# Moving the SiLU-derivative passes of a backward kernel, and weaving one weight-gradient block into the transform

## The chip, the core and the metric

The kernel runs on one core of a Trainium2 chip. The metric is device time in microseconds (us) of one execution; lower is better. The engines named below are TensorE (PE, matmuls), its weight loads (PEld), VectorE (DVE), ScalarE (ACT), GpSimd (POOL) and SyncE (SP), which here only issues DMA transfers. Each engine takes its own list of instructions in order. A tile framework builds these lists ahead of time from the program's dependencies, its priorities and explicit `issue_after` edges, so the order of the source is not always the order on an engine.

## What is computed

The program is the forward and backward pass of four residual blocks: two long-convolution blocks (done by FFT) and two dense blocks with SiLU, in turn.

```python
def _B_ref(x, w1, w2):
    h = jnp.einsum("bsd,df->bsf", x, w1)      # S=2048, D=448, F=1792
    h = _silu(h)
    return jnp.einsum("bsf,fd->bsd", h, w2)

x = A_q
x = x + _A_ref(_layernorm(x), A_k, A_v, A_shift_k, A_ssm_k, A_ssm_D)   # long convolution
x = x + _B_ref(_layernorm(x), B_w1, B_w2)                              # dense, "layer 1"
x = x + _A_ref(_layernorm(x), A_k, A_v, A_shift_k, A_ssm_k, A_ssm_D)
x = x + _B_ref(_layernorm(x), B_w1, B_w2)                              # dense, "layer 2"

_out, _vjp = jax.vjp(_f, A_q, A_k, A_v, A_shift_k, A_ssm_k, A_ssm_D, B_w1, B_w2)
return (_out, *_vjp(grad_out))
```

In the backward pass of a dense block, the gradient at the hidden layer is `(g @ w2.T) * silu'(h)`. The kernel keeps the pre-activation `h` (tiles `dT`; for layer 1 stored to memory as `DT_d` and loaded back as `dTl`) and turns it into `silu'(h)` in place with an ACT pass, the "derivative pass".

## The kernel before

The sequence is cut into four chunks of 512 rows. `L == 1` is layer 2, `L == 0` is layer 1. For each chunk of the backward pass, `ga` forms `g @ w2.T` (matmuls into `ps_g`, an ACT copy to `ghp`, a DVE multiply with the derivative into `ghT`), and `gn` multiplies by `w1.T` (matmuls into `ps_n`, evacuated by ACT into `lb_u0`) and runs the layer-norm gradient on DVE, for four row tiles `tl`. `g_pre` transposes the incoming gradient on PE (`ps_t`) and copies it out (`gT`).

```python
    def slope(self, d):                       # derivative passes over one half chunk
        for o in range(0, 7, 2):
            n = min(2, 7 - o)
            self.nc.scalar.activation(d[:, o:o + n, :], d[:, o:o + n, :], ACT.Derivative_silu)
        self.k.bal.add("act", 3.4)

    def h(self, c, L, nT, half, hold, pre=None):
        ...                                   # pre-activations in ps_h; ACT: Silu into aT; DVE: copy into dT
            last = nc.scalar.activation(a, ps[:, 0:n, :], ACT.Silu)
        ...
        if L == 1:
            if half == 1:
                with self.tc.issue_after(last.ins):
                    for _, d in hold:
                        self.slope(d)

    def ga(self, c, L, gT, dT, mid=None, loads=(None, None)):
        ...
        for fp in range(NF // 2):             # 7 pairs of hidden blocks
            ps = k.psum.tile([P, 2, 512], FP32, name="ps_g", tag="mm", bufs=2)
            self.contract(ps, self.w2T, gT, 2 * fp, 2, ...)
            gh = self.ch.tile([P, 2, 512], BF16, name="ghp", tag="ghp", bufs=2)
            k.last_gh = nc.scalar.copy(gh[:], ps[:])
            if fp == 2 and mid:
                with self.tc.issue_after(k.last_gh.ins):
                    mid()
            ...                               # DVE: ghT = dT * gh
            if fp in (3, 6):
                hh = (fp - 3) // 3
                if loads[hh]:
                    ld.append(self.load_d(*loads[hh]))      # dTl <- DT_d, three buffers "D"
                self.store_turned(k.GH_d[L], ghT[hh], c, hh)  # DMA transposes on SP's queue

    def gn(self, c, L, ghT, nb, gres, na):
        for tl in range(4):
            pn = k.psum.tile([P, 512], FP32, name="ps_n", ...)
            for ft in range(NF):
                nc.tensor.matmul(pn[:, :D], lhsT=ghT[ft // 7][...], rhs=self.w1T[:, ft, :], ...)
            u0 = self.ch.tile([P, D], FP32, name="lb_u0", tag="lb_u0", bufs=2)
            last_u = nc.scalar.activation(u0[:], pn[:, :D], ACT.Identity, scale=..., accum_out=...)
            if tl == 1:
                k.mid_u = last_u
            ...                               # DVE: layer-norm gradients (ln_bwd twice), gYb

    def run(self):
        ...
        for c in range(4):                    # layer 2, forward end and backward
            gb, gT = self.g_pre(c, 1, gb_next if c else self.g_load(0))
            d0 = self.h(c, 1, nT, 1, cur, (lambda: self.load_d(0, 0)) if c == 3 else None)
            ...
            self.out(c, cur, True)
            ...
            if c == 3:
                self.slope(d0)
            ...                               # ga(c, 1, ...)
            if c == 3:
                ...
                nl = self.load_n(0)
                gn = self.g_pre(0, 0)
            self.gn(c, 1, ghT, nb, lambda tl: gb[:, tl, :], na)
        for c in range(4):                    # layer 1, backward
            with self.tc.issue_after(k.mid_u.ins):
                self.slope(d1)
            ...
            ghT = self.ga(c, 0, gT, dT, (lambda: self.slope(e0)) if c < 3 else None, ...)
            if c < 3:
                ...
                gn = self.g_pre(c + 1, 0)
            self.gn(c, 0, ghT, nb, lambda tl: self.X[:, 4 * c + tl, :], na)
```

After that comes the suffix: the FFT of the gradient `gYb` and the weight gradients. `_gw2` is a generator of matmuls (`ps_d`), 32 for each of 14 blocks of the gradient of `w2`; `_gw1` does the same for `w1`. `weave(n)` places `n` of these matmuls on PE between pieces of the transform, and the rest is drained near the end.

```python
        for _ in _gw2(k, k.dp, range(1), [(k.dp, "dstat", 3)], first=k.go_jobs.ins):
            pass                              # the first block, in one piece

        def jobs():
            yield from _gw2(k, k.dp, range(1, NF), both)
            yield from _gw1(k, dp2, both)
        ...
        for n2 in range(16):                  # first stage of the transform: 2 matmuls, 1 copy each
            with _in_turn(k):
                _fft_stage1(k, n2, k.gYb[:, n2, :], A1, psum, nc.scalar if n2 < 12 else None)
            weave(2 if n2 < 8 else 8 if n2 < 12 else 12)
```

Of the kernel before, what the change touches and what calls it, by code (L numbers as in the profile page):

```python
# [12 lines left out]
ACT = mybir.ActivationFunctionType  # L13
# [451 lines left out]
class Main:  # L465
# [91 lines left out]

    def slope(self, d):
        for o in range(0, 7, 2):
            n = min(2, 7 - o)  # L560
            self.nc.scalar.activation(d[:, o:o + n, :], d[:, o:o + n, :], ACT.Derivative_silu)  # L561
        self.k.bal.add("act", 3.4)

# [99 lines left out]

    def gn(self, c, L, ghT, nb, gres, na):
        nc, k = self.nc, self.k
# [4 lines left out]
        for tl in range(4):  # L670
            t = 4 * c + tl
            pn = k.psum.tile([P, 512], FP32, name="ps_n", tag="tr" if L == 1 and tl % 2 else "po", bufs=2)
            for ft in range(NF):
                nc.tensor.matmul(pn[:, :D], lhsT=ghT[ft // 7][:, ft % 7, tl * P:(tl + 1) * P], rhs=self.w1T[:, ft, :], start=(ft == 0), stop=(ft == NF - 1))  # L674
            u0 = self.ch.tile([P, D], FP32, name="lb_u0", tag="lb_u0", bufs=2)
            last_u = nc.scalar.activation(u0[:], pn[:, :D], ACT.Identity, scale=k.rstd[2 * L + 1][:, t:t + 1], accum_out=cp[:, tl, 0:1])  # L676
# [38 lines left out]
    def run(self):  # L715
        k, nc = self.k, self.nc
        pairs = ((0, 2), (2, 4))
        with self.tc.high_priority():
            self.a_fwd(0, 0, k.x0c0, k.na0, pairs)
            nT = self.b_tr(self.b_pre(0, 1, pairs, nc.vector))  # L720
        cur = []
        self.h(0, 0, nT, 0, cur)
        for c in range(4):
# [13 lines left out]
        for c in range(4):  # L737
# [10 lines left out]
            if c == 3:  # L748
                self.slope(d0)
            box = []  # L750
            if c < 3:
                ghT = self.ga(c, 1, gT, cur, lambda: box.append(self.b_pre(c + 1, 3)))
            else:
                ghT, d1, e0 = self.ga(c, 1, gT, cur, None, ((0, 1), (1, 0)))
# [5 lines left out]
            else:  # L760
                k.GO = k.wk.tile([P, NT, D], BF16, name="GO", tag="WA")
                k.go_jobs = k.d_load
                nl = self.load_n(0)
                gn = self.g_pre(0, 0)
            self.gn(c, 1, ghT, nb, lambda tl: gb[:, tl, :], na)
            na, nb = na1, nb1
        for c in range(4):
            with self.tc.issue_after(k.mid_u.ins):
                self.slope(d1)
            dT, (nb, na), (gb, gT) = ((None, d0), (None, d1)), nl, gn  # L770
            ghT = self.ga(c, 0, gT, dT, (lambda: self.slope(e0)) if c < 3 else None, ((c + 1, 1) if c < 3 else None, (c + 2, 0) if c < 2 else None))
# [32 lines left out]
def _job(k, ps, src, ft, mov, slot, start, stop, first=None):  # L804
# [6 lines left out]
    for t in range(NT):  # L811
        i = k.nc.tensor.matmul(ps[:, :D], lhsT=st[:, t, :], rhs=mov[:, t, :], start=start and t == 0, stop=stop and t == NT - 1)  # L812
        k.pe_engine = i.ins.engine
        yield i
# [46 lines left out]
def _ssm_suffix(k):  # L861
# [7 lines left out]
    with ExitStack() as es:  # L869
# [229 lines left out]
```

## Time and profile before

| what | value |
|---|---|
| device time, median of 3 runs | 764.16 us (762.78 to 764.94) |
| span of the profiled execution | 764.7 us |
| PE busy | 714.1 us (93%) |
| DVE busy | 510.2 us (67%) |
| ACT busy | 459.6 us (60%) |
| mean granted TensorE clock | 0.984 of full speed |

A busy share is an average over stages; what a stage is limited by is read from that stage's own time line. In such a line stand the start in us from the start of the span, the length in us, the engine, the source line and operation, the tile written and the tile read, how many instructions were merged, and in square brackets the idle time before it with the engine and operation that ended it. The stage of this change lies between about 357 us (the end of layer 2's third chunk) and 548 us (the end of the transform's first stage).

### The profile page before, as it was taken

The numbers are of one execution on the slowest core, as the hardware profiler recorded it, in microseconds if no ns is written. First come the engines' busy times: TensorE is split into PE (matmuls) and PEld (weight loads), VectorE is DVE, ScalarE is ACT, GpSimd is POOL, SyncE is SP. The second block draws the span as 40 slices with busy tenths as digits, with TensorE's granted clock in tenths as the row PEclk, the third lists the DMA queues.
The fourth block names the chain that finished last, engine by engine and source line by source line (L and its number), as shares of the span: only waits on it lengthen the run. The fifth ranks groups of instructions, "written<-read, shape, count | busy, mean of one in ns | idle before, by whom it ended". The sixth has DMA issues, their size and how long they took to land.

```text
span 764.7 us, 12731 instructions
## 1 busy us (share of the span) xinstructions
PE 714.1 (93%) x5025; PEld 380.8 (50%) x5025; DVE 510.2 (67%) x1061; ACT 459.6 (60%) x576; POOL 101.3 (13%) x168
## 2 busy tenths in 40 slices
PE   6998879999999999999799899997989999899997
PEld 4876533444444443434344344443656675555554
DVE  3789868788733796966748889894287753269600
ACT  3878867666557487686786779736357664111111
POOL 1034312222100001000000000001111122112210
PEclk9999989999999999999899999999999999999999
DMA  9449999999879999869589999999739778587761
GB/s 302 154 137 273 354 278 311 294 289 246 208 155 247 196 251 221 180 157 220 140 208 288 219 317 288 190 303 295 263 108 402 258 254 284 160 285 233 222 187 46
DMA packets 188504, 180.17 MB, mean 236 GB/s; under 512 B 136155, under 2 KB 164703, under 8 KB 187293
## 3 DMA queue, kind: packets, MB, share of 16 engines
q1 hardware_dynamic: 174736, 122.21, 62.3%
q0 software_dynamic: 12784, 54.64, 20.3%
q10 hardware_dynamic: 924, 2.52, 1.0%
q8 instruction: 39, 0.64, 0.3%
q14 instruction: 21, 0.16, 0.1%
HBM read 76.66 MB, written 65.87 MB: 186 GB/s over the span
## 4 chain that ended last, share of the span: by engine, by line
PE 53%; DVE 25%; ACT 9%; DMA 6%; issue 5%; POOL 1%; SPq 0%; DVEq 0%; ACTq 0%; POOLq 0%
PE ps_d L812 20%; PE ps_o L601 8%; PE ps_h L519 7%; DVE lb_junk L649 3%; DVE dT L113 3%; PE ps_n L674 2%; DVE lb_u L660 2%; PE ps_g L519 2%; PE ps_v L232 2%; PE ps_v L231 2%; DVE ghT L636 2%; DVE ln_st L259 2%; DMA turned<-ghT 2%; ACT na L273 2%; DVE lb_u L689 2%
## 5 line engine op out<-in xcount | busy, mean ns | idle before, releaser
L812 PEld LDWEIGHTS <-dstat 128*128 128x128 bf16 x896 | 85.7, 99 | 76.9 <-issue 4.0
L519 PE MATMUL ps_h<-nT,w1sb 128*128 128x512 bf16 (+1 forms) x448 | 104.7, 387 | 2.6 <-DVE dT L113 1.4
L519 PE MATMUL ps_g<-gT,w2T 128*128 128x512 bf16 (+1 forms) x448 | 94.1, 380 | 3.6 <-ACT ghp L628 3.4
L674 PE MATMUL ps_n<-w1T,ghT 128*128 128x448 bf16 x448 | 89.5, 353 | 4.0 <-DVE ghT L636 3.7
L601 PE MATMUL ps_o<-w2sb,aT 128*128 128x448 bf16 x448 | 92.3, 357 | 0.2 <-ACT aT L576 0.2
L812 PE MATMUL ps_d<-mov,dstat 128*128 128x448 bf16 x448 | 87.2, 352 | 0.3 <-DMA mov<-N_d 0.3
L576 ACT ACTIVATE aT<-ps_h 128x1024 bf16<-128x1024 f32 (+1 forms) x64 | 58.5, 918 | 42.6 <-PE ps_h L519 33.9
L113 DVE CAST dT<-ps_h 128x1024 bf16<-128x1024 f32 (+1 forms) x56 | 59.5, 1066 | 32.1 <-ACT aT L576 32.1
L519 PEld LDWEIGHTS <-w1sb 128*128 128x128 bf16 (+1 forms) x448 | 36.4, 97 | 66.3 <-issue 38.2
L519 PEld LDWEIGHTS <-w2T 128*128 128x128 bf16 (+1 forms) x448 | 35.1, 97 | 62.1 <-issue 29.1
L674 PEld LDWEIGHTS <-ghT 128*128 128x128 bf16 x448 | 42.4, 98 | 46.5 <-DVE ghT L636 6.7
L628 ACT CAST ghp<-ps_g 128x1024 bf16<-128x1024 f32 x56 | 55.3, 1009 | 15.5 <-PE ps_g L519 10.5
L601 PEld LDWEIGHTS <-aT 128*128 128x128 bf16 x448 | 42.4, 99 | 43.7 <-issue 6.5
L812 PE MATMUL ps_d<-GO,dstat 128*128 128x448 bf16 x224 | 53.8, 367 | 1.9 <-DMA dstat<-A_d 1.9
L812 PE MATMUL ps_d<-X,dstat 128*128 128x448 bf16 x224 | 50.9, 352 | 0.0
L856 ACT CAST dout<-ps_d 128x448 bf16<-128x448 f32 x14 | 7.5, 532 | 58.2 <-PE ps_d L812 58.2
L676 ACT ACTIVATE lb_u<-ps_n,rstd 128x448 f32<-128x448 f32 x32 | 20.3, 633 | 32.6 <-DVE X L661 13.7
L231 PEld LDWEIGHTS <-pa 128*128 128x128 bf16 x336 | 33.5, 100 | 10.2 <-DVE pa L443 6.6
L232 PEld LDWEIGHTS <-pb 128*128 128x128 bf16 x336 | 33.2, 100 | 8.9 <-DVE pb L444 4.2
L561 ACT ACTIVATE dTl<-dTl 128x1024 bf16<-128x1024 bf16 (+1 forms) x32 | 28.6, 939 | 7.7 <-DMA dTl<-DT_d 7.6
L636 DVE TENSOR_TENSOR ghT<-dT,ghp 128x1024 bf16<-128x1024 bf16 (+1 forms) x32 | 19.5, 619 | 20.1 <-ACT ghp L628 19.9
L602 DVE TENSOR_TENSOR X<-X,ps_o 128x448 bf16<-128x448 bf16 x32 | 19.7, 615 | 16.6 <-PE ps_o L601 16.6
(192 smaller groups left out, 1212.0 us busy)
## 6 DMA issues: line engine op xcount, KB each, us to landing
GH_d<-turned SPq DMA_DIRECT2D x16, 896.0 KB, 5.2
dstat<-A_d SPq DMA_DIRECT2D x28, 512.0 KB, 5.9
dstat<-GH_d SPq DMA_DIRECT2D x28, 512.0 KB, 4.0
A_d<-turned SPq DMA_DIRECT2D x12, 896.0 KB, 4.8
DT_d<-dT POOLq DMA_DIRECT2D x8, 896.0 KB, 5.8
dTl<-DT_d SPq DMA_DIRECT2D x8, 896.0 KB, 6.6
spec_K<-Z POOLq DMA_DIRECT2D x7, 512.0 KB, 7.8
KB<-Z POOLq DMA_DIRECT2D x14, 256.0 KB, 12.0
```

What stands on the lines that cost most here:

```text
L113: eng.tensor_copy(out, in_)
L231: nc.tensor.matmul(pv[:, i, :], lhsT=pa[:, i * P:(i + 1) * P], rhs=k.Gsb[:, ga, :], start=True, stop=False)
L232: nc.tensor.matmul(pv[:, i, :], lhsT=pb[:, i * P:(i + 1) * P], rhs=k.Gsb[:, gb, :], start=False, stop=True)
L519: self.nc.tensor.matmul(ps[:, u, :], lhsT=w[lo:hi, b, f:f + P], rhs=x[lo:hi, b, :], start=(seen[u] == 1), stop=(seen[u] == ND))
L561: self.nc.scalar.activation(d[:, o:o + n, :], d[:, o:o + n, :], ACT.Derivative_silu)
L576: last = nc.scalar.activation(a, ps[:, 0:n, :], ACT.Silu)
L601: nc.tensor.matmul(po[:, :D], lhsT=aT[ft // 7][0][:, ft % 7, tl * P:(tl + 1) * P], rhs=self.w2sb[:, ft, :], start=(ft == 0), stop=(ft == N ...
L628: k.last_gh = nc.scalar.copy(gh[:], ps[:])
L636: nc.vector.tensor_tensor(out=ghT[hh][:, o:o + len(u), :], in0=dT[hh][1][:, o:o + len(u), :], in1=gh[:, u[0]:u[0] + len(u), :], op=ALU.mult)
L649: nc.vector.scalar_tensor_tensor(out=junk[:], in0=u0, scalar=1.0, in1=n_t, op0=ALU.mult, op1=ALU.mult, accum_out=cp[:, 1:2])
L674: nc.tensor.matmul(pn[:, :D], lhsT=ghT[ft // 7][:, ft % 7, tl * P:(tl + 1) * P], rhs=self.w1T[:, ft, :], start=(ft == 0), stop=(ft == NF - 1))
L812: i = k.nc.tensor.matmul(ps[:, :D], lhsT=st[:, t, :], rhs=mov[:, t, :], start=start and t == 0, stop=stop and t == NT - 1)
```

## The change

Three things are moved; no arithmetic is added or taken away.

1. The derivative passes on `d0`, the first half chunk of layer 1, are held behind the last derivative pass of layer 2 (`k.last_slope`). Before, nothing but the data held them, and the built order had them among the last SiLU evacuations of layer 2.
2. In the backward pass of layer 1, the four passes over a half chunk are no longer issued in a block. Those on `d1` go one behind each `lb_u0` evacuation of `gn`; those on `e0` (the first half of the next chunk) go one behind the `ghp` copies of pairs 1, 2, 4 and 5. The transposes of the next chunk's gradient (`g_pre`) go behind the `ps_n` matmuls of `tl == 1` instead of ahead of `gn`.
3. The first `w2` block joins the other jobs: its 32 matmuls are no longer one piece ahead of the transform. The first 12 steps of the transform are given 4 job matmuls each (before: 2 for each of 8 steps, 8 for each of 4).

```diff
-    def slope(self, d):
-        for o in range(0, 7, 2):
-            n = min(2, 7 - o)
-            self.nc.scalar.activation(d[:, o:o + n, :], d[:, o:o + n, :], ACT.Derivative_silu)
-        self.k.bal.add("act", 3.4)
+    def slope(self, d, pieces=range(4)):
+        for o in pieces:
+            n = min(2, 7 - 2 * o)
+            s = d[:, 2 * o:2 * o + n, :]
+            self.k.last_slope = self.nc.scalar.activation(s, s, ACT.Derivative_silu)
+            self.k.bal.add("act", 0.5 * n)
@@ ga
-            if fp == 2 and mid:
+            if mid:
                 with self.tc.issue_after(k.last_gh.ins):
-                    mid()
+                    mid(fp)
@@ gn
-            if tl == 1:
-                k.mid_u = last_u
+            k.pe_engine = mm.ins.engine
+            if hook:
+                hook(tl, mm.ins, last_u.ins)
@@ run
+        def hook(c, d):
+            def run(tl, mm, u):
+                with self.tc.issue_after(u):
+                    self.slope(d, (tl,))
+                if tl == 1:
+                    with self.tc.issue_after(mm):
+                        box.append(self.g_pre(c, 0))
+            return run
@@
             if c == 3:
-                self.slope(d0)
+                with self.tc.issue_after(k.last_slope.ins):
+                    self.slope(d0)
@@
-                gn = self.g_pre(0, 0)
-            self.gn(c, 1, ghT, nb, lambda tl: gb[:, tl, :], na)
+            self.gn(c, 1, ghT, nb, lambda tl: gb[:, tl, :], na, None if c < 3 else hook(0, d1))
@@
-            with self.tc.issue_after(k.mid_u.ins):
-                self.slope(d1)
...
-            ghT = self.ga(c, 0, gT, dT, (lambda: self.slope(e0)) if c < 3 else None, ...)
+            ghT = self.ga(c, 0, gT, dT, (lambda fp: self.slope(e0, {1: (0,), 2: (1,), 4: (2,), 5: (3,)}.get(fp, ()))) if c < 3 else None, ...)
             if c < 3:
...
-                gn = self.g_pre(c + 1, 0)
-            self.gn(c, 0, ghT, nb, lambda tl: self.X[:, 4 * c + tl, :], na)
+            self.gn(c, 0, ghT, nb, lambda tl: self.X[:, 4 * c + tl, :], na, hook(c + 1, d1) if c < 3 else None)
@@ _ssm_suffix
-        for _ in _gw2(k, k.dp, range(1), [(k.dp, "dstat", 3)], first=k.go_jobs.ins):
-            pass
         def jobs():
+            yield from _gw2(k, k.dp, range(1), [(k.dp, "dstat", 3)], first=k.go_jobs.ins)
             yield from _gw2(k, k.dp, range(1, NF), both)
@@
-            weave(2 if n2 < 8 else 8 if n2 < 12 else 12)
+            weave(4 if n2 < 12 else 12)
```

More of the change, by code (lines that the diff above doesn't have):

```diff
@@ L662, in ln_bwd, with gn @@
         self.k.bal.add("dve", 2.0)
-    def gn(self, c, L, ghT, nb, gres, na):
+    def gn(self, c, L, ghT, nb, gres, na, hook=None):
         nc, k = self.nc, self.k
@@ L673, in gn @@
             for ft in range(NF):
-                nc.tensor.matmul(pn[:, :D], lhsT=ghT[ft // 7][:, ft % 7, tl * P:(tl + 1) * P], rhs=self.w1T[:, ft, :], start=(ft == 0), stop=(ft == NF - 1))
+                mm = nc.tensor.matmul(pn[:, :D], lhsT=ghT[ft // 7][:, ft % 7, tl * P:(tl + 1) * P], rhs=self.w1T[:, ft, :], start=(ft == 0), stop=(ft == NF - 1))
             u0 = self.ch.tile([P, D], FP32, name="lb_u0", tag="lb_u0", bufs=2)
@@ L721, in run @@
         cur = []
+        box = []
+        def hook(c, d):
[6 more added lines that the diff above has]
+            return run
         self.h(0, 0, nT, 0, cur)
@@ L748, in run @@
             if c == 3:
-                self.slope(d0)
+                with self.tc.issue_after(k.last_slope.ins):
+                    self.slope(d0)
             box = []
             if c < 3:
-                ghT = self.ga(c, 1, gT, cur, lambda: box.append(self.b_pre(c + 1, 3)))
+                ghT = self.ga(c, 1, gT, cur, lambda fp: box.append(self.b_pre(c + 1, 3)) if fp == 2 else None)
             else:
@@ L763, in run @@
                 nl = self.load_n(0)
-                gn = self.g_pre(0, 0)
-            self.gn(c, 1, ghT, nb, lambda tl: gb[:, tl, :], na)
+            self.gn(c, 1, ghT, nb, lambda tl: gb[:, tl, :], na, None if c < 3 else hook(0, d1))
             na, nb = na1, nb1
         for c in range(4):
-            with self.tc.issue_after(k.mid_u.ins):
-                self.slope(d1)
-            dT, (nb, na), (gb, gT) = ((None, d0), (None, d1)), nl, gn
-            ghT = self.ga(c, 0, gT, dT, (lambda: self.slope(e0)) if c < 3 else None, ((c + 1, 1) if c < 3 else None, (c + 2, 0) if c < 2 else None))
+            dT, (nb, na), (gb, gT) = ((None, d0), (None, d1)), nl, box.pop()
+            ghT = self.ga(c, 0, gT, dT, (lambda fp: self.slope(e0, {1: (0,), 2: (1,), 4: (2,), 5: (3,)}.get(fp, ()))) if c < 3 else None, ((c + 1, 1) if c < 3 else None, (c + 2, 0) if c < 2 else None))
             if c < 3:
@@ L812, in _job @@
         i = k.nc.tensor.matmul(ps[:, :D], lhsT=st[:, t, :], rhs=mov[:, t, :], start=start and t == 0, stop=stop and t == NT - 1)
-        k.pe_engine = i.ins.engine
         yield i
```

## The prediction

> **What bounds the kernel now.** I began with the busy line of the page: PE 93%, DVE 67%, ACT 60%. PE is the engine to keep fed, so I looked for its idle time between 357 and 548 us, the stretch that the change touches. The page's list of costly groups has one striking entry, an ACT line that waits for a DMA:
>
> ```profile
> L561 ACT ACTIVATE dTl<-dTl 128x1024 bf16<-128x1024 bf16 (+1 forms) x32 | 28.6, 939 | 7.7 <-DMA dTl<-DT_d 7.6
> ```
>
> Nearly all idle time ahead of the derivative passes is one wait of 7.6 us. ACT's time line shows where it is:
>
> ```profile
> 356.67 0.64 ACT L676 ACTIVATE lb_u<-ps_n,rstd 128x448 f32<-128x448 f32 x1
> ...
> 357.42 1.28 ACT L561 ACT_TABLE_LOAD   x1
> 366.30 1.06 ACT L561 ACTIVATE dTl<-dTl 128x1024 bf16<-128x1024 bf16 x1 [7.60 <-DMA dTl<-DT_d]
> 367.27 0.62 ACT L676 ACTIVATE lb_u<-ps_n,rstd 128x448 f32<-128x448 f32 x1
> ...
> 368.82 1.00 ACT L111 COPY gT<-ps_t 128x1024 bf16<-128x1024 bf16 x1
> 369.84 1.28 ACT L576 ACT_TABLE_LOAD   x1
> ```
>
> A derivative pass on d0 stands in ACT's list ahead of an lb_u evacuation and a gT copy that were ready long before, and its data lands only at 366.3. PE's time line of the same place shows what that costs:
>
> ```profile
> 362.21 2.10 PE L519 MATMUL ps_h<-nT,w1sb 128*128 128x512 bf16 x8
> 369.87 1.01 PE L530 MATMUL ps_t<-ident,gb 128*128 128x128 bf16 x8 [5.56 <-ACT gT L111]
> 370.68 1.60 PE L519 MATMUL ps_h<-nT,w1sb 128*128 128x512 bf16 x4
> 372.21 3.45 PE L601 MATMUL ps_o<-w2sb,aT 128*128 128x448 bf16 x10
> ```
>
> PE stands for 5.56 us, and then it is slow: ten ps_o matmuls in 3.4 us (372.21 to 375.59), where 39 of them take 7.4 us a little later (0.19 us each). The granted clock from 366.3 to 375 us is 0.61. DVE stood 5.24 us here too, for the same late lb_u.
>
> The third view is the table by stretches, one row per chunk, cut where the first lb_u of a chunk starts (columns: stretch, length, then busy us of PE, PEld, DVE, ACT, POOL, the clock, the DMA share, GB/s):
>
> ```profile
> 402.93:429.22 26.29, 24.31 (x135) 11.07 (x134) 23.87 (x60) 18.12 (x25) 0.00 (x0) 1.00 0.98 254
> 429.22:455.45 26.23, 24.60 (x135) 11.08 (x134) 22.73 (x64) 20.85 (x29) 0.54 (x1) 1.00 1.04 287
> 455.45:480.93 25.48, 23.69 (x130) 10.53 (x129) 22.83 (x64) 20.82 (x29) 0.54 (x1) 1.00 1.06 287
> 480.93:504.87 23.94, 22.11 (x111) 9.23 (x110) 22.03 (x63) 15.71 (x24) 0.00 (x0) 1.00 1.11 242
> ```
>
> A chunk needs of PE 56 ps_g at 0.207, 56 ps_n at 0.188 and 16 transposes (0.9), 23.0 us. DVE needs 22 to 24. The chunk takes 24 to 26. So two engines are nearly full and the chunk's dependency loop (last ghT multiply, ps_n, lb_u, layer norm) costs the rest. The last place is the start of the suffix, on PE:
>
> ```profile
> 526.18 0.54 PE L211 MATMUL ps_s<-gYb,M1s 128*128 128x448 bf16 x2 [0.59 <-ACT A1g L111]
> 528.63 3.17 PE L812 MATMUL ps_d<-GO,dstat 128*128 128x448 bf16 x8 [1.92 <-DMA dstat<-A_d]
> ```
>
> [...]
>
> **Part 1, d0 behind layer 2's passes.** I compared the built orders. ACT before has LoadActFuncSet five times in this stretch (357.42, 369.84, 374.19, 376.56 and 381.41 in the trace), after only once, ahead of layer 2's own passes. I walk the new order with the old durations.
> - PE ends ps_n at 361.8, then transposes and ps_h run on without the stall, as gT's copy needs only the transposes: two ps_h groups done by 365.2.
> - The third ps_h group waits for DVE's dT copy of the first (about 365.9), done 367.6; the fourth for the second's (about 368.7), done 370.4. DVE is 5.2 us earlier than before, as its wait is gone.
> - 49 ps_o at 0.189: 379.7. There ps_g starts, which was at 387.65: 8.0 us gained, of which 5.6 are the stall and about 2.4 the slow clock.
> - ACT: the last Silu 371.4, table load to 372.7, eight passes of layer 2 (6.8) to 379.5, the four of d0 (0.87 x 3 + 0.52 = 3.1) to 382.5. The first ghp is needed when two ps_g groups of 1.65 us fill both buffers, at 383.0; it ends 383.4. A stall of 0.4.
> - ps_g ends 391.7. The 16 transposes (0.9) are no longer ahead of ps_n, so the first lb_u is at 394.4, where it was 402.93. **Gain so far: 8.5 us.**
>
> **Part 2, passes singly.** ACT's work is the same 3.1 us per half chunk. What changes is the end of ga. Between the fourth lb_u of one chunk and the last ghp copy, ACT had 11.8 us before in the second chunk (442.24 to 454.07), with four passes, and both gT copies in between; in the new order 10.5 (the gT copies, 1.9, now behind tl 1 in gn, where ACT has slack). DVE waited 0.51 + 1.14 for these ghp, and 0.5 + 0.2 in the next chunk.
> - Layer 2's last chunk: DVE's 24.2 us from 395.1 end at 419.4; next first lb_u at 420.0 (was 429.22), gain 9.2.
> - First chunk of layer 1: walking ACT, ghp 7 ends at 443.8, multiply, ps_n, lb_u at 445.0 (was 455.45): 10.4.
> - Second chunk: here a pass on d1 stands behind the first lb_u, ahead of gT and the second lb_u. In the trace d1's load is issued at 452.08, 3.4 us ahead of the first lb_u, and lands 7.3 us later, so 3.9 us behind it. Pass 0.87, gT 0.9: the second lb_u would start at 5.7, where DVE wants it by about 4.6. The load hangs behind transposes in SP's queue (one takes 8.87 us at 443.09, after GO's 1.8 MB), so it moves less than the rest. I charge 2 us: gain 8 to 9 at 472.
> - Third chunk: the load lands 3.8 us behind the first lb_u (476.81 + 7.9); I charge 0.4. **Gain at the first lb_u of the last chunk: 8.5 to 9.**
>
> **Part 3, the first w2 block.** In the old times ps_n ends at 511.4. Before, 32 ps_d (6.05 us) follow, then the steps, to 548.1, with 0.33 + 1.06 + 0.59 + 1.92 us of idle time and 1.5 of slow clock. After, the steps start at once, but ACT's first A1g copy stands behind the third lb_u, at DVE's pace of 4.7 us per tile (507.98, 512.72, 517.46). The third step waits to 514.4 (0.7), the fourth to 516.7 (1.2), the sixth 0.3; then 12 steps with 4 ps_d each are done at 527.6 and four with 12 at 538.3. 32 ps_d are left over for the end, 6.05 us: 544.4 against 548.1, a gain of 3.7. The third and fourth dstat loads follow the last transposes on SP (518.78), which may hold the 13th step by about 1 us. **Gain 2.7.**
>
> Sum: 8.75 + 2.7 = 11.5; 764.16 - 11.5 = 752.7, rounded to 752.5.
>
> **Rivals.**
> - *DMA takes over.* For: the DMA share is 0.98 to 1.16 in all four chunk rows, and the lag from the last ghT multiply to the issue of the last transpose grows, 4.8, 6.9, 10.7 us in three chunks. If compute comes 9 us early and transfers do not, loads of d1 and dstat come late each time. Against: 366 to 395 us has shares of 0.42 to 0.73, so the transfers move forward as well. Then 757 to 759.
> - *The new waits at d1 eat part 2 wholly,* 2 us in each of three chunks: 756.
> - *The loop closes well:* no wait at d1, chunks at DVE's 23 us, no dstat wait: 764 - 8.5 - 4 - 3.7 = 748.
> - *Nothing gained:* the stall comes back as a stall of ps_g for the longer block of passes. Against: that block is 3.1 us longer, four table loads (5.1 us) shorter.
>
> **Range and chances.** The 8 us of the stall stand on a wait that cannot return. The rest is +4 to -3. Range 747.5 to 758. Two percent is 748.9: faster 0.2, same 0.78, slower 0.02.
>
> **What would show it.** Right: no ACT wait for DT_d near 357, no PE gap over 1 us from there to ps_g, one table load, clock 1.0; ps_g of layer 2's last chunk 8 us earlier; the first lb_u at about 394, 420, 445 and 472. Part 2 wrong: ACT waiting for dTl behind the first lb_u of a chunk with DVE waiting for lb_u, or chunks longer than before. Part 3 wrong: more than 3 us of PE idle between ps_n's end and the 16th step, by A1g or dstat.

## The result, and the profile after

| version | median, us | ratio to before, 95% interval |
|---|---|---|
| before | 763.47 (762.18 to 764.94, 4 runs) | 1 |
| the change | 753.82 (753.61 to 757.78, 4 runs) | 0.9885 (0.9847 to 0.9923) |

The change takes 9.65 us off, 1.15%; the interval lies wholly below 1. The predicted time was 752.5 us. The ratios, here and below, leave out the few executions that fell into a slower state (up to 779.8 us); the medians do not.

Runs start shifted against each other by some microseconds (more on this at the end), so all readings below are taken from a mark that both kernels share: the second `lb_u` evacuation of layer 2's third chunk, at 356.67 us in the trace of before and at 356.75 in that of the change. The first thing to look for is the derivative passes in the page's list of costly groups. This is the row of the changed kernel (after the bar: busy us, mean ns of one; then idle us ahead and what ended it):

```profile
L562 ACT ACTIVATE dTl<-dTl 128x1024 bf16<-128x1024 bf16 (+1 forms) x32 | 29.8, 946 | 2.2 <-DMA dTl<-DT_d 2.2
```

The idle time ahead of these passes fell from 7.7 to 2.2 us. It is not gone, though. ACT's time line of the changed kernel (start, length, engine, line, operation, tiles, count, idle time ahead) shows what became of the old wait and where the new one is:

```profile
356.75 0.64 ACT L677 ACTIVATE lb_u<-ps_n,rstd 128x448 f32<-128x448 f32 x1
361.04 0.63 ACT L677 ACTIVATE lb_u<-ps_n,rstd 128x448 f32<-128x448 f32 x1 [3.56 <-DVE X L662]
362.50 1.01 ACT L111 COPY gT<-ps_t 128x1024 bf16<-128x1024 bf16 x1 [0.73 <-PE ps_t L530]
...
371.57 1.28 ACT L562 ACT_TABLE_LOAD   x1
372.86 6.83 ACT L562 ACTIVATE dT<-dT 128x1024 bf16<-128x1024 bf16 x8
379.59 3.45 ACT L562 ACTIVATE dTl<-dTl 128x1024 bf16<-128x1024 bf16 x4
382.95 1.90 ACT L629 CAST ghp<-ps_g 128x1024 bf16<-128x1024 f32 x2
...
472.26 0.63 ACT L677 ACTIVATE lb_u<-ps_n,rstd 128x448 f32<-128x448 f32 x1 [1.37 <-PE ps_n L675]
...
474.90 1.06 ACT L562 ACTIVATE dTl<-dTl 128x1024 bf16<-128x1024 bf16 x1 [1.91 <-DMA dTl<-DT_d]
```

The third `lb_u`, at 367.27 before, now runs at 361.04, and the `gT` copy at 362.50 instead of 368.82. One table load stands where five stood, and twelve derivative passes run in a row (eight on layer 2, four on d0). The new wait is at 474.90: the first pass on d1, which the change put behind the first `lb_u` of a chunk, waits 1.91 us for its load.

PE's time line of the changed kernel, in the place where before had its gap of 5.56 us:

```profile
370.42 9.50 PE L602 MATMUL ps_o<-w2sb,aT 128*128 128x448 bf16 x49
379.75 3.40 PE L519 MATMUL ps_g<-gT,w2T 128*128 128x512 bf16 x15
383.99 8.25 PE L519 MATMUL ps_g<-gT,w2T 128*128 128x512 bf16 x39 [0.85 <-ACT ghp L629]
```

All 49 ps_o matmuls run at 0.19 us each, and the granted clock from 366.3 to 375 us is 1.00 (before 0.61), so the slow clock is gone with the gap. ps_g starts at 379.75 instead of 387.65. What is left is a stall of 0.85 us, at the place where the row of twelve passes keeps the first `ghp` copy waiting.

The table by stretches of the changed kernel, one row per chunk from first `lb_u` to first `lb_u` (stretch, length, busy us of PE, PEld, DVE, ACT, POOL, the clock, DMA share, GB/s), answers to the four rows shown of before:

```profile
395.03:420.68 25.65, 23.84 (x129) 10.59 (x130) 23.80 (x60) 18.11 (x25) 0.00 (x0) 1.00 1.01 272
420.68:446.47 25.79, 23.85 (x129) 10.70 (x130) 22.69 (x64) 20.77 (x30) 0.54 (x1) 1.00 1.06 311
446.47:472.26 25.79, 24.21 (x131) 10.78 (x132) 22.69 (x64) 20.81 (x29) 0.54 (x1) 1.00 1.05 255
472.26:497.73 25.47, 22.53 (x123) 10.09 (x124) 22.66 (x64) 17.35 (x25) 0.00 (x0) 1.00 1.10 271
```

The four chunks took 26.29, 26.23, 25.48 and 23.94 us; they take 25.65, 25.79, 25.79 and 25.47. The first two became 1.1 us shorter in sum, the last two 1.8 us longer. So part 2, which was meant to shorten the chunks, gained nothing over the four. "The last chunk" is here and below the fourth of these rows; its place in time is the third chunk of layer 1. Last, the start of the suffix on PE in the changed kernel:

```profile
505.48 0.54 PE L211 MATMUL ps_s<-gYb,M1s 128*128 128x448 bf16 x2
...
509.59 0.54 PE L211 MATMUL ps_s<-gYb,M1s 128*128 128x448 bf16 x2 [0.54 <-ACT A1g L111]
...
520.58 2.43 PE L822 MATMUL ps_d<-GO,dstat 128*128 128x448 bf16 x12
...
530.79 1.06 PE L914 MATMUL ps_tr<-ident,A1g 128*128 128x128 bf16 x16
```

One wait of 0.54 us is left among the sixteen steps, and the 13th step runs into its job matmuls (520.58) without a wait for `dstat`.

**The balance of the two traces.** The first ps_tr, which ends the stage, is at 548.10 before and at 530.79 after, with 32 ps_d (6.05 us) fewer done by then: 17.31 - 6.05 = 11.26 us gained. The spans differ by 13.1 (764.7 and 751.6). Of the other 1.85 us, the visible part is a PE gap within the `ps_sk` matmuls of the suffix and the slow matmuls behind it (granted clock 0.59 from 661.18 to 665.3 us), before:

```profile
661.18 1.49 PE L1035 MATMUL ps_sk<-kx_s,gks 128*32 128x128 bf16 x37 [2.23 <-issue]
662.60 2.76 PE L812 MATMUL ps_d<-GO,dstat 128*128 128x448 bf16 x7
```

and after ("issue" means that the profile shows nothing that PE waited for; the clock is 1.00 from 644.26 to 646 us):

```profile
644.26 0.33 PE L1043 MATMUL ps_sk<-kx_s,gks 128*32 128x128 bf16 x5 [1.50 <-issue]
644.52 1.50 PE L822 MATMUL ps_d<-GO,dstat 128*128 128x448 bf16 x7
```

Part 3 has a hand in this, as the experiments show. The profiled execution of before took 766.83 us, 2.7 more than the 764.16 given for that kernel at the outset, so these two traces show somewhat more than the medians' 9.65.

### The profile page after: what moved, and what is told of

It is laid out like the page before. It is cut to its first block, busy times and chain, and to the rows that moved or that the text cites. A ratio compares the mean times of both kernels' runs of the same rounds, so it can differ in the third digit from the quotient of the medians.

```text
span 751.6 us, 12677 instructions
## 1 busy us (share of the span) xinstructions
PE 704.3 (94%) x4980; PEld 378.1 (50%) x5025; DVE 509.8 (68%) x1061; ACT 453.8 (60%) x572; POOL 101.0 (13%) x168
## 4 chain that ended last, share of the span: by engine, by line
PE 53%; DVE 24%; ACT 13%; issue 5%; DMA 4%; POOL 1%; SPq 0%; DVEq 0%; ACTq 0%; POOLq 0%
PE ps_d L822 20%; PE ps_h L519 8%; PE ps_o L602 6%; PE ps_n L675 3%; DVE lb_junk L650 3%; DVE dT L113 3%; DVE lb_u L661 2%; PE ps_v L232 2%; PE ps_g L519 2%; PE ps_v L231 2%; DVE ln_st L259 2%; DVE ghT L637 2%; ACT na L273 2%; DVE lb_u L691 2%; ACT ghp L629 1%
## 5 line engine op out<-in xcount | busy, mean ns | idle before, releaser
L519 PE MATMUL ps_h<-nT,w1sb 128*128 128x512 bf16 (+1 forms) x432 | 102.4, 385 | 4.2 <-DVE dT L113 1.4
L822 PE MATMUL ps_d<-GO,dstat 128*128 128x448 bf16 x224 | 51.4, 352 | 0.2
```

The source lines that it names most:

```text
L519: self.nc.tensor.matmul(ps[:, u, :], lhsT=w[lo:hi, b, f:f + P], rhs=x[lo:hi, b, :], start=(seen[u] == 1), stop=(seen[u] == ND))
```

## Experiments

Twelve runs were made, of eleven new kernels and of the changed one once more. All traces were cut at the same marks:

- **A**: from the shared mark to the first `lb_u` of layer 2's last chunk;
- **chunks**: the four lengths from first `lb_u` to first `lb_u`: layer 2's last chunk, then the first, second and third of layer 1;
- **T**: from the first `lb_u` of layer 1's last chunk to the first ps_tr, less 6.05 us where the first w2 block lies inside it;
- **sum**: A, the chunks and T together. It leaves out what lies ahead of the mark and behind the stage.

| kernel | parts | median us | ratio to before (95%) | A | chunks | T | sum |
|---|---|---|---|---|---|---|---|
| before | - | 763.47 | 1 | 46.26 | 26.29 26.23 25.48 23.94 | 37.18 | 185.4 |
| the change | 1 2 3 | 753.82 | 0.9885 (0.9847-0.9923) | 38.28 | 25.65 25.79 25.79 25.47 | 33.06 | 174.0 |
| change_again | 1 2 3 | 754.18 | 0.9894 (0.9860-0.9928) | 38.28 | 25.66 25.77 25.80 26.63 | 33.06 | 175.2 |
| p1_only | 1 | 755.98 | 0.9902 (0.9884-0.9919) | 39.05 | 26.30 26.23 25.48 23.93 | 34.53 | 175.5 |
| p3_only | 3 | 761.06 | 0.9977 (0.9950-1.0003) | 45.21 | 26.30 26.23 25.49 23.93 | 32.29 | 179.5 |
| no_p1 | 2 3 | 763.30 | 0.9998 (0.9982-1.0013) | 45.33 | 25.65 25.78 25.79 28.28 | 33.06 | 183.9 |
| no_p3 | 1 2 | 758.59 | 0.9939 (0.9914-0.9964) | 38.27 | 25.66 25.80 25.79 27.55 | 34.88 | 178.0 |
| p1p3 | 1 3 | 752.55 | 0.9878 (0.9850-0.9907) | 39.05 | 26.30 26.23 25.48 23.94 | 32.80 | 173.8 |
| d1_late | 1 2' 3 | 755.18 | 0.9893 (0.9877-0.9909) | 38.28 | 25.91 25.80 25.82 25.47 | 33.05 | 174.3 |
| gpre_early | 1 2' 3 | 754.59 | 0.9882 (0.9848-0.9915) | 38.27 | 25.47 25.79 26.40 25.40 | 33.05 | 174.4 |
| tables | 1' 2 3 | 759.38 | 0.9969 (0.9947-0.9991) | 42.37 | 25.66 25.79 25.80 25.35 | 33.06 | 178.0 |
| gpre_before | 1 2' 3 | 753.20 | 0.9873 (0.9840-0.9905) | 39.05 | 24.93 25.97 26.35 23.90 | 33.03 | 173.2 |
| p1p3_d0ga | 1' 3 | 752.59 | 0.9857 (0.9824-0.9890) | 38.30 | 26.31 26.23 25.47 23.93 | 32.69 | 172.9 |
| p1p3_d0ga_e0 | 1' 2' 3 | 751.75 | 0.9849 (0.9812-0.9885) | 38.32 | 24.53 26.15 25.99 24.35 | 33.36 | 172.7 |

A prime marks a part in another form. The trace figures repeat far better than the times: the four chunks of p1_only, p1p3 and before agree within 0.01 us. Ratios are compared across groups of runs, and medians only within one group. A kernel was executed 4 to 20 times.

### The parts, one by one and one left out

**p1_only** is the kernel before with nothing but the hold on d0:

```diff
-            self.nc.scalar.activation(d[:, o:o + n, :], d[:, o:o + n, :], ACT.Derivative_silu)
+            self.k.last_slope = self.nc.scalar.activation(d[:, o:o + n, :], d[:, o:o + n, :], ACT.Derivative_silu)
@@
-                self.slope(d0)
+                with self.tc.issue_after(k.last_slope.ins):
+                    self.slope(d0)
```

> The kernel before with d0's passes held behind layer 2's last ones and nothing else. Theory (the stall is the gain, parts add up): the first lb_u of layer 2's last chunk comes 8 us earlier and the lead lasts to the end, 8 us off, about 755.5 us. Rival (DMA takes over): the lead is there at that lb_u but shrinks in the chunks that follow, as transposes and loads do not come earlier by as much; 3 to 5 us off, about 759.5. Rival (the passes singly are what makes the lead last): as the DMA one.

Measured: ratio 0.9902, 7.5 us of 763.7. A fell from 46.26 to 39.05, by 7.2 us, and the chunks stayed as they were (T is shorter too; see part 3 below). So part 1 is most of the change, its gain is made ahead of layer 2's last chunk, and no later wait takes it back.

**p3_only** is the kernel before with nothing but the first w2 block woven in:

```diff
-        for _ in _gw2(k, k.dp, range(1), [(k.dp, "dstat", 3)], first=k.go_jobs.ins):
-            pass
         def jobs():
+            yield from _gw2(k, k.dp, range(1), [(k.dp, "dstat", 3)], first=k.go_jobs.ins)
@@
-            weave(2 if n2 < 8 else 8 if n2 < 12 else 12)
+            weave(4 if n2 < 12 else 12)
```

> The kernel before with only the first w2 block woven into the transform. Theory: the gaps of 3.9 us and the slow clock of 1.5 us after ps_n mostly go, 4 us off, about 759.5 us, with no stall of ps_d by dstat over 0.5 us. Rival (the 4 us seen in the trace of the change come from the earlier transfers of part 1, not from the weave): the dstat wait stays, 1 to 2 us off, about 762.

Measured: ratio 0.9977, 1.8 us where 4 were expected, with an interval that reaches 1. T fell by 4.9 us against the trace of before, and the `dstat` wait to 0.20 us.

**no_p1** is the change with `self.slope(d0)` not held; **no_p3** is the change with the lines of part 3 as they were before.

> The changed kernel without the hold on d0 (parts 2 and 3 alone). Theory: the 5.6 us PE gap near 364 us and the slow clock are back, 8 us slower than the change, about 762 us. Rival (part 2 gives a good part): 758 us or less.

> The changed kernel with the first w2 block in one piece again, weave as before (parts 1 and 2 alone). Theory: 4 us slower than the change, about 758 us; together with the run of part 1 alone it gives part 2: if part 2 costs about 1 us, part 1 alone is 1 us faster than this. Rival (part 2 gains 1 to 2 us as predicted): this is 1 to 2 us faster than part 1 alone.

Measured: without part 1 the gain is gone, 0.9998. A is back at 45.33, and the last chunk is 2.8 us longer than with the whole change. Without part 3 the ratio is 0.9939; T rose by 1.8, and the last chunk by 2.1 us, although the order of instructions up to there is that of the change. Both long chunks have the same cause, a longer wait for d1, which is taken up below.

**p1p3** is the kernel before with parts 1 and 3 and without part 2 (the two diffs above together).

> The kernel before with parts 1 and 3 (hold on d0, first w2 block woven), the derivative passes of layer 1 in blocks as before. Theory (part 2 costs 2 to 3 us, by p1_only against no_p3): 7.5 from part 1 and 2 to 4 from part 3, ratio to before 0.985 to 0.9875, about 753 us, as fast as the full change or 1 to 2 us faster. Rival (part 2 is what makes part 3 worth 4 us): ratio 0.990 to 0.992, slower than the change by 1 to 3 us.

Measured: 752.55 us, ratio 0.9878, against 0.9885 and 0.9894 for the change in its two groups of runs. The sum of the marks is 173.8, against 174.0 and 175.2. Part 2 therefore brings nothing that can be seen. Parts 1 and 3 alone make 7.5 + 1.8 = 9.3 us, and together they make 1.22% of 763.1, 9.3 us: they add up, as far as intervals of 1.3 to 2.2 us to either side can tell.

Part 3's own share is best read from p1p3 against p1_only, which differ in it alone. PE's time line of p1_only:

```profile
513.87 0.54 PE L211 MATMUL ps_s<-gYb,M1s 128*128 128x448 bf16 x2 [0.33 <-ACT A1g L111]
...
515.85 0.54 PE L211 MATMUL ps_s<-gYb,M1s 128*128 128x448 bf16 x2 [1.07 <-ACT A1g L111]
...
520.59 0.54 PE L211 MATMUL ps_s<-gYb,M1s 128*128 128x448 bf16 x2 [0.60 <-ACT A1g L111]
522.05 1.69 PE L813 MATMUL ps_d<-GO,dstat 128*128 128x448 bf16 x8 [0.92 <-DMA dstat<-A_d]
```

and of p1p3:

```profile
506.77 0.54 PE L211 MATMUL ps_s<-gYb,M1s 128*128 128x448 bf16 x2 [0.46 <-ACT A1g L111]
...
519.92 2.44 PE L814 MATMUL ps_d<-GO,dstat 128*128 128x448 bf16 x12 [0.72 <-DMA dstat<-A_d]
```

The waits of p1_only sum to 2.92 us, those of p1p3 to 1.18. The difference, 1.74, is the difference in T (34.53 - 32.80 = 1.73). That is part 3 inside the marks: 32 matmuls laid mostly over waits for `A1g`.

Before itself had 2.65 us more in T than p1_only, whose order there is the same. Its `dstat` wait was 1.92 instead of 0.92, and eight ps_d after it took 3.17 us in the time line instead of 1.69 (granted clock 0.68 from 528.6 to 534 us, in p1_only 1.00 from 511 to 540): 1.0 + 1.5 = 2.5. In no_p3, the third kernel with this order, T is 34.88. Whether the shift of 7 us by part 1 removes this wait, or whether it differs from execution to execution, one trace of each can't tell.

Behind the marks something else goes with part 3. In the traces of before and of the change the `ps_sk` gap shown above comes when 581 of PE's recorded matmuls are left. Part 3 sends 32 `ps_d` past that point, so that the gap comes 32 `ps_sk` matmuls later. It is 2.23 and 2.26 us in before and p1_only, without part 3, and 1.50, 1.32 and 0.85 us in the change, p1p3 and change_again, with it. From the first ps_tr to the end the three traces without part 3 (before, p1_only, no_p3) take 215.0 to 216.6 us, and the eleven with it 213.7 to 214.8, once the 6.05 us of the 32 matmuls are taken off. The means are 1.9 us apart, so part 3 may be worth more than its 1.7 us. The medians (1.8 us in p3_only) are too coarse to say, and what makes the gap was not varied.

### What the table loads cost

Part 1 takes away two things at once: the wait for d0's load and four table loads. To separate them, **tables** keeps the hold on d0 and puts a tiny derivative pass (4 elements a row) behind the first and third of layer 2's last four SiLU evacuations. That makes five table loads in the stretch, as before, with no pass that waits for a transfer:

```diff
+            if L == 1 and c == 3 and half == 1 and ft0 in (7, 10):
+                with self.tc.issue_after(last.ins):
+                    nc.scalar.activation(k.warm[:], k.mhalf[:], ACT.Derivative_silu)
```

> The full change, with two tiny derivative passes (4 elements a row) behind the first and third of layer 2's last four SiLU passes, so that ACT loads its table five times there as before, and waits for no DMA. If the four table loads were part of part 1's gain: 4 x 1.3 us on ACT delay the eight passes and the first ghp copy by 3 to 5 us, PE's stall ahead of ps_g's third group grows from 0.85 to about 3 us, 2 to 3 us slower than the change. Theory (the stall was the DMA wait alone, ACT has slack between the SiLU passes): the loads fall into ACT's gaps of 0.4 to 1.7 us, under 1 us slower.

ACT's time line of tables:

```profile
365.18 1.28 ACT L580 ACT_TABLE_LOAD   x1
366.47 0.20 ACT L580 ACTIVATE warm<-mhalf 128x4 f32<-128x4 f32 x1
366.58 0.99 ACT L111 COPY gT<-ps_t 128x1024 bf16<-128x1024 bf16 x1
367.60 1.28 ACT L577 ACT_TABLE_LOAD   x1
...
375.31 1.28 ACT L562 ACT_TABLE_LOAD   x1
```

and PE's:

```profile
381.06 3.40 PE L519 MATMUL ps_g<-gT,w2T 128*128 128x512 bf16 x15
387.73 9.71 PE L519 MATMUL ps_g<-gT,w2T 128*128 128x512 bf16 x39 [3.27 <-ACT ghp L632]
```

A rose from 38.28 to 42.37: 4.1 of the 8.0 us come back with the loads alone, more than I had expected. The four loads are 5.1 us of ACT's list, and ACT is what ps_g waits for here: the stall grows from 0.85 to 3.27 us (2.4), ps_g starts a little later, and after the stall 39 matmuls take 9.71 us instead of 8.25 (1.5). The ratio, 0.9969, is higher than the change's by 6 us, with intervals that allow 1.8 and more. So the kernel with five loads and without the wait for the transfer gains 3.9 us over before in A, and the one with a single load gains 8.0: once the wait is gone, the order of two functions on ACT decides half of the gain. It does not follow that the loads were half of what before lost: there PE lost its 8.0 us ahead of ps_g, with no second gap, and a kernel with the wait and a single load was not run.

### The wait for d1

In the change, d1's first pass stands behind the first `lb_u` of a chunk and ahead of a `gT` copy and the second `lb_u`. **d1_late** keeps part 2 but puts no pass behind the first `lb_u`:

```diff
-                    self.slope(d, (tl,))
+                    self.slope(d, ((), (0,), (1,), (2, 3))[tl])
```

> The full change, with the four passes on d1 behind the second, third and twice the fourth lb_u of a chunk instead of one behind each. Theory (what part 2 loses is the pass behind the first lb_u, which waits for d1's load with gT and the second lb_u behind it): no ACT wait for DT_d over 0.5 us, no PE wait for lb_u in the third chunk of layer 1, that chunk 25.5 us long as at best; 1 to 2 us faster than the change. Rival (the order of ps_g loses it): unchanged within 0.5 us.

Measured: no pass waits for its load any more, but the expected 1 to 2 us did not come: the last chunk is 25.47 us, to the hundredth that of the change with its wait of 1.91. This does not yet tell what the wait costs, because d1_late also has another order on ACT (both `gT` copies ahead of the second `lb_u`, the passes crowded behind). Runs with one order and different waits tell it. **change_again** is the changed kernel, run once more beside the last three variants.

> The changed kernel itself, beside the three variants on the same chip. Expected 753 to 755 us; the wait for d1's load in the third chunk of layer 1 between 1.5 and 4.7 us by run. If the wait is what spreads the times, a run with a wait of over 4 us is 1.5 us or more above one with a wait under 2 us; if it is not, the times agree whatever the wait.

ACT's time line of change_again:

```profile
473.57 0.63 ACT L677 ACTIVATE lb_u<-ps_n,rstd 128x448 f32<-128x448 f32 x1 [1.37 <-PE ps_n L675]
...
477.38 1.06 ACT L562 ACTIVATE dTl<-dTl 128x1024 bf16<-128x1024 bf16 x1 [3.08 <-DMA dTl<-DT_d]
```

and of no_p1:

```profile
478.82 0.63 ACT L677 ACTIVATE lb_u<-ps_n,rstd 128x448 f32<-128x448 f32 x1 [1.37 <-PE ps_n L675]
...
484.27 1.06 ACT L562 ACTIVATE dTl<-dTl 128x1024 bf16<-128x1024 bf16 x1 [4.72 <-DMA dTl<-DT_d]
```

Who feels the wait is seen on DVE, here in the trace of the change:

```profile
480.02 0.39 DVE L657 TENSOR_TENSOR G<-G,lb_v 128x448 bf16<-128x448 bf16 x1 [0.88 <-ACT lb_v L655]
```

The pass `lb_v` (a step of the layer-norm gradient) stands in ACT's list behind the waiting pass, both `gT` copies, the second `lb_u` and the second pass, and DVE stands until it comes. The five kernels below have the same order on ACT up to there. The third column sums DVE's gaps in the second row tile (in the last three it waits for the second `lb_u` too):

| kernel | wait for d1, us | DVE's gaps, us | last chunk, us | last chunk less gaps |
|---|---|---|---|---|
| tables | 1.80 | 0.77 | 25.35 | 24.58 |
| the change | 1.91 | 0.88 | 25.47 | 24.59 |
| change_again | 3.08 | 1.95 | 26.63 | 24.68 |
| no_p3 | 4.00 | 2.86 | 27.55 | 24.69 |
| no_p1 | 4.72 | 3.59 | 28.28 | 24.69 |

DVE's gaps are the wait less 1.0 to 1.1 us, and the chunk grows with them, microsecond by microsecond. So about 1 us of wait is free for DVE, and the 1.91 of the change were not. Whether the chunk would lose all of the 0.88 with a shorter wait isn't shown, as no run of this order had one below 1.80. In d1_late DVE has no gap at this place but two near the end, 0.48 and 0.51 us for `ghp` copies. In the second chunk of layer 1, where `lb_v` comes ahead of the second `gT` copy, waits of 0.33 to 1.66 us left the length at 25.8.

What moves the wait is the moment at which the load is issued. SyncE's queue in the trace of the change:

```profile
462.49 5.75 SPq L485 DMA_TRANSPOSE turned<-ghT  x1
468.34 0.54 SPq L700 DMA_DIRECT2D dTl<-DT_d  x1
```

and of no_p3:

```profile
464.08 5.91 SPq L485 DMA_TRANSPOSE turned<-ghT  x1
470.08 0.53 SPq L700 DMA_DIRECT2D dTl<-DT_d  x1
```

In both kernels the first `lb_u` is at 472.26, so the load goes out 3.92 us ahead of it in one and 2.18 in the other, each time at the end of a transpose in the same queue. It lands after 6.5 and 6.9 us. In change_again it is 2.86 ahead and 6.6. Why the transposes end at other times in one run than in another wasn't settled. Whether this wait also explains the spread of the run times stays open: change_again's profiled run, with 1.17 us more wait, took 755.15 us against 753.80, but part of that lies ahead of the mark, and no run of this kernel had a wait of over 4 us.

### The late transposes

The change moves the next chunk's gradient transposes from ahead of `gn` to behind its second row tile. The last chunk is 1.5 us longer with it, with a wait for d1 (the change) or without (d1_late). **gpre_early** puts the transposes behind the first row tile (`if tl == 0`), and **gpre_before** puts them back ahead of `gn`, with the passes still taken singly:

```diff
-                if tl == 1:
-                    with self.tc.issue_after(mm):
-                        box.append(self.g_pre(c, 0))
@@ run, layer 2's last chunk
+                box.append(self.g_pre(0, 0))
@@ run, layer 1
+                box.append(self.g_pre(c + 1, 0))
```

> The full change, with the next chunk's transposes behind the first row tile's ps_n matmuls instead of the second's. Theory (DMA wait): the wait stays, 0 to 1 us slower. Rival (the late gT delays ps_g and the last chunk, 25.5 us against 23.9): the last chunk back to about 24 us, 1 to 1.5 us faster.

> The change, with the next chunk's gradient transposes put back ahead of the w1 product (as before the change), the passes still taken singly. Theory (the late transposes, which keep PE from filling the holes between the last groups of ps_g, stretch the last chunk of layer 1): the last chunk comes back from 25.5 us to about 24.0 between its first lb_u and the one before, and layer 2's last chunk's first lb_u comes about 0.8 us later; the middle chunks 25.5 to 26.3; time within 1 us of the change. Rival (the single passes stretch it): the last chunk stays at 25.5 us, and the time is 1 us above the change.

Measured: behind the first row tile the last chunk is 25.40 us, not the 24 that were hoped for; ahead of `gn` it is 23.90, as before the change. A is longer by 0.77 us there, since the transposes are in it again. PE's time line of gpre_before in the last chunk, whose first `lb_u` is at 473.98:

```profile
480.54 3.40 PE L519 MATMUL ps_g<-gT,w2T 128*128 128x512 bf16 x16
484.47 6.72 PE L519 MATMUL ps_g<-gT,w2T 128*128 128x512 bf16 x32 [0.54 <-ACT ghp L629]
492.15 1.78 PE L519 MATMUL ps_g<-gT,w2T 128*128 128x512 bf16 x8 [0.96 <-ACT ghp L629]
```

and of the change, first `lb_u` at 472.26:

```profile
480.18 3.40 PE L519 MATMUL ps_g<-gT,w2T 128*128 128x512 bf16 x15
485.20 5.01 PE L519 MATMUL ps_g<-gT,w2T 128*128 128x512 bf16 x24 [1.62 <-ACT ghp L629]
490.84 3.41 PE L519 MATMUL ps_g<-gT,w2T 64*128 64x512 bf16 x15 [0.63 <-ACT ghp L629]
```

With the transposes early, ps_g begins 6.56 us after the first `lb_u` and ends after about 20.0; with the transposes late it begins after 7.92 and ends after about 22.0. Of the 1.36 us at the start, 0.9 are the 16 transposes themselves. Ahead of `gn` each set stands at the end of the row before (in the trace of before the last set ran at 470.04, and the last chunk has none); in the change A has none and the last chunk has a set, with its two `gT` copies on ACT. PE's waits for `ghp` grow from 1.5 to 2.25 us, and DVE, which has no gap after the first `lb_u` in gpre_before, stands 0.88 us for `lb_v` and 0.46 for a `ghp` copy in the change. So it is the place of the transposes, not the single passes, that lengthens the last chunk. The place also buys 0.77 us in A. In the chunks between, the two forms differ by -0.7, +0.2 and +0.6 us, the last with a wait for d1 of 2.87 us in that run, so over all marks they come to 173.2 against 174.0.

### A better version of the same ideas

The stall of 0.85 us (0.73 in p1p3) ahead of the third ps_g group was put down to the twelve passes in a row. **p1p3_d0ga** is p1p3 with d0's four passes singly behind the `ghp` copies of pairs 1, 2, 4 and 5 of layer 2's last `ga`. **p1p3_d0ga_e0** does the same with e0's passes in layer 1. d1's passes stay in a row behind the second `lb_u`, and the transposes ahead of `gn`:

```diff
-                with self.tc.issue_after(k.last_slope.ins):
-                    self.slope(d0)
@@
-                ghT, d1, e0 = self.ga(c, 1, gT, cur, None, ((0, 1), (1, 0)))
+                ghT, d1, e0 = self.ga(c, 1, gT, cur, lambda fp: self.slope(d0, {1: (0,), 2: (1,), 4: (2,), 5: (3,)}.get(fp, ())), ((0, 1), (1, 0)))
@@ p1p3_d0ga_e0 alone
-            ghT = self.ga(c, 0, gT, dT, (lambda fp: self.slope(e0) if fp == 2 else None) if c < 3 else None, ...)
+            ghT = self.ga(c, 0, gT, dT, (lambda fp: self.slope(e0, {1: (0,), 2: (1,), 4: (2,), 5: (3,)}.get(fp, ()))) if c < 3 else None, ...)
```

> The kernel before with the hold on d0 and the woven first w2 block (no single passes in layer 1), but with d0's four passes taken singly behind the ghp copies of pairs 1, 2, 4 and 5 of layer 2's last chunk, instead of in a row ahead of them. Theory (the stall of 0.7 to 0.85 us ahead of the third ps_g group is ACT's row of passes): the stall goes, the first lb_u of layer 2's last chunk comes 0.7 us earlier, and the time is 0.5 to 1 us under that of the two parts alone (752.5 on the run before this one). Rival (the passes delay the ghp copies behind them by as much): stalls of 0.3 to 0.5 us at the later ps_g groups, and the time is unchanged.

> The same, and e0's passes in layer 1 singly behind the ghp copies of pairs 1, 2, 4 and 5 too; d1's passes stay in a row behind the second lb_u, the transposes stay ahead of the w1 product. Theory (the single passes on e0 are the harmless half of part 2, as no load stands behind them; what part 2 loses are the late transposes and d1's early places): chunks of 25.6 to 26.0, 25.5 and 25.5 us and a last one of 24, time 0.5 to 1 us under the one without. Rival (part 2 is worth nothing in either half): chunks of 26.3, 26.2 and 25.5 as before, the time the same within 0.5 us.

PE's time line of p1p3_d0ga:

```profile
368.73 9.50 PE L602 MATMUL ps_o<-w2sb,aT 128*128 128x448 bf16 x49
378.06 11.62 PE L519 MATMUL ps_g<-gT,w2T 128*128 128x512 bf16 x56
```

All 56 ps_g now run in one piece, so the row of passes was the stall. A falls from 39.05 to 38.30, the 0.75 us expected. With e0 singly too, the chunks did not come as expected: the first of the four falls to 24.53 us and the two last rise by 0.5 and 0.4, a net gain of 0.9 on the chunks, of which T gives 0.7 back. The medians of this group are 751.75 and 752.59 us, beside 754.18 for the change and 762.11 for before. They are the two lowest ratios of the study, 0.9849 and 0.9857. Their intervals overlap the change's, so only the marks (172.7 and 172.9 against 174.0 and 175.2) say that they beat it, and between the two there is nothing to choose. Passes taken singly are thus worth 0.75 us on d0, where no load stands behind them; on e0 they do no harm, and a gain isn't shown.

## Why the prediction was right, and which steps failed

**Part 1 was right in its mechanism and its size.** No ACT wait near 357, one table load, no PE gap over 1 us, ps_g at 379.75 where 379.7 was predicted. The gain at the first `lb_u` of layer 2's last chunk is 402.93 - 395.03 = 7.9 us, predicted 8.5. The term that was mis-sized is ACT's row of passes: the four of d0 take 3.36 us (379.59 to 382.95), not 3.1, and begin 0.1 late, so the stall is 0.85 instead of 0.4. The split of the 8.0 us into 5.6 for the stall and 2.4 for the slow clock is right for where PE lost them. The table loads stood only in the last rival, as 5.1 us against the 3.1 of the longer row of passes; the run tables shows how much hung on them: with five loads in the new order, 4.1 of the 8.0 us would have been lost again, ahead of the third ps_g group.

**Part 2 failed as a gain.** The gains at the first `lb_u` of the following chunks were predicted as 9.2, 10.4, 8 to 9 and 8.5 to 9; they are 8.5, 9.0, 8.7 and 7.1. Three of its steps went wrong:

- *The first chunk of layer 1* was to take 25.0 us and took 25.79. Moving the `gT` copies out of ACT's tail and taking the passes singly saved 0.4 us against before, not 1.2.
- *The waits at d1* were charged with 2 us in the second chunk and 0.4 in the third. In the trace of the change the waits there are 0.33 and 1.91 us, and they cost nothing and up to 0.9. The rule behind the charge was that DVE wants the second `lb_u` 4.6 us after the first. That holds (it started at 4.50 in the change, and DVE had no gap there), but the step stopped at this instruction: DVE waited 0.88 us for `lb_v`, further down in ACT's list. What could not be known from one trace is the landing. It came 1.0 and 2.6 us after the first `lb_u`, not 3.9 and 3.8; in change_again it was 2.4 and 3.8, and there the last chunk was 1.16 us longer than in the change.
- *The last chunk* was given no loss for the late transposes. They cost 1.5 us there (gpre_before), and that is where the gain at 504.87 fell to 7.1. The step saw that the transposes leave A and ACT's tail, and not that a set of them then stands in the last chunk, which had none.

The rival "the new waits at d1 eat part 2 wholly" named the right outcome, no gain from part 2, but of the cause only a part: a wait cost something in one chunk of the three, and the transposes were not in it.

**Part 3 was larger against the trace of before than predicted, and smaller by itself.** Predicted 2.7; between before and the change T fell by 37.18 - 33.06 = 4.1 us. Of that, 2.5 us are before's `dstat` wait and the slow clock after it, in excess of p1_only; the step counted the loss of them as gain, and then charged 1 us for a `dstat` wait in the new order that did not come (0 in the change, 0.72 in p1p3, so it does occur). The three predicted waits of 0.7, 1.2 and 0.3 came as one of 0.54: PE came to its first step 1.2 us later in the chunk than it would have before (7.75 us after the first `lb_u`, where ps_n ended after 6.53), so it had less to wait for. Beside p1_only the part's own worth inside the marks is 1.7 us.

**The sum held, in part by luck.** 11.45 us were predicted and 11.26 stand between the two traces at the first ps_tr: part 2 too high by about 1.6 us at the last `lb_u` (8.75 less 7.1), part 3 too low by 1.4. The two errors cancelled, and neither knew of the other. By the medians the gain is 9.65; the profiled execution of before was 2.7 us above its median, as said. The rival in which DMA takes over (757 to 759) is out for the whole, since the DMA share in the chunks stayed where it was (1.01 to 1.10, before 0.98 to 1.11) and the loads moved forward with the compute. The rival of a loop that closes well (748) is out because the chunks did not come to DVE's 23 us.

## What to carry to other kernels

An instruction that waits for a transfer and stands in an engine's list ahead of ready work held up the whole list here: ACT stood 7.60 us with an `lb_u` and a `gT` copy behind the pass, and PE 5.56 us for that copy. Hold such an instruction behind what must not wait, and group the calls of one function while doing so (here one table load of 1.28 us stands where five stood). Before such a pass is put at an earlier place, work out how late its data may land there without cost (here about 1 us of wait), and compare that with the spread of the landing over several runs (here 2.6 and 3.8 us after the `lb_u` in two runs of one kernel), not with one trace. When work is moved off a full stretch, count it at the place where it goes: the transposes cost 1.5 us in the last chunk and saved 0.77 ahead of the first.

## What was not expected of the hardware

- **The start of a stretch moves from run to run.** The shared mark, up to which PE's list is the same in before and in the change, was at 354.4 us in one trace and at 361.2 in another, fourteen traces in all. That is more than half of what the change gains, and why marks inside the trace tell apart what the times can't.
- **Whether a gap slows PE's clock is not a matter of its length alone.** Fourteen ps_n took 4.49 us after a gap of 2.87 us in no_p1 (granted clock 0.88 from 478.82 to 490 us), and 2.81 us, as long as the fourteen ahead of the gap, after one of 2.15 in no_p3. In before, eight ps_d took 3.17 us after a gap of only 1.92 us, with 0.59 us of idle time and two matmuls ahead of it; eight in p1_only took 1.69 after a gap of 0.92. And the `ps_sk` gaps, 2.23 us in before and 2.26 in p1_only, were followed by seven ps_d in 2.76 and 2.73 us, the one of 1.50 in the change by seven in 1.50. What decides beside the length is not shown, as no run here varied it.
- **A table load took 1.28 us of ACT and left no gap.** In tables a load starts at 365.18, 0.02 us after the pass ahead of it ends, and the next pass starts at 366.47, 1.29 us after the load's start.
